# A fused attention and two-MoE kernel: its opening's loads, queue places and low parts rearranged

## The chip, the cores and the metric

The kernel runs on one core of a Trainium2 chip (trn2). The metric is device time in microseconds (us); lower is better. The median of three runs before the change is 1096.28 us (1095.65 to 1096.59).

## The reference

Attention over B = 4 batches, H = 8 heads, S = 576 positions and D = 64, with a memory read beside it, then two gated feed-forward layers on the 2304 x 512 result:

```python
scores = where(causal, -1e9, q @ k.T / sqrt(D)); a = softmax(scores); local = a @ v
q_p = phi(q)                                   # phi(x) = elu(x) + 1
mem_out = (q_p @ M_prev) / (q_p @ z_prev + 1e-6)
x = g * mem_out + (1 - g) * local              # g = sigmoid(beta), one per head
x = (sigmoid(x @ w_gate) * (x @ w_val)) @ w_out       # layer 1: 512 -> 1536 -> 512
out = ((x @ w_a) * (x @ w_b)) @ w_out2                # layer 2: 512 -> 1536 -> 512
```

The feed-forward weights and `setup_inputs` are float64; everything else and the output is float32.

## The kernel before

The attention part works on 16 pairs of heads, four pairs to a batch; pair p is one turn of the loop at L668. A turn interleaves three pairs: the scores, row maxima and exponentials of pair p, the transposes and normalisation of pair p-1, and the product with v of pair p-2. All of it is float32. What a turn does, by function:

- `load_q`, `load_k` (through `load_rows`, L104), `load_v`, `load_z`: three, three, four and one DMA for a pair. Before the loop (L661 to L667) q, k, z and v of pair 0 are loaded and its q and k transposed (`turn`, `turn4`).
- `scores` (L184): six products on TensorE for row blocks X = (0, 2, 3), later six for Y = (1, 4), into one PSUM tile `sc` per head. Y uses the place of X, so it waits until X has been read.
- `expo` (L207): VectorE adds the mask and takes the row extreme (L223), ScalarE takes the exponential with a row sum (L228), GpSimd copies 64 columns of each block into `mix` (L233).
- `phi1` (L239): `e` = exp(min(q, 0)) by VectorE L242 and ScalarE L243, `qp` by VectorE L245, then `e` = qp * z on GpSimd L248. `phi2` (L255): the norm sums on VectorE (L258 to L264). `qp` and `e` have one buffer each.
- `sums` (L267): once all exponentials of pair p-1 are done, VectorE forms the factors (L274, L280, L289) and GpSimd scales `qp` into `mix` (L284, two halves).
- `turn_w`, `turn_mix`, `pv`, `spread`: transposes of the probabilities (tiles `aw`) and of `mix`, products with v, and the way of 1/sum through DRAM back to 64 partitions.

While this runs, layer 1 is prepared. `w_piece` (L389) turns a float64 weight block into float32 and then into a high part (fp32r) and a low part: DMA into `st`; VectorE L402 and ScalarE L406; VectorE L408, L411 and GpSimd L414; ScalarE L417 (high part) and GpSimd L418 (low part). `w_stream` works on 12 such pieces; `fill(p)` (L639) calls one step (two from pair 4 on), three times a turn from p = 1 on. `split_a` (L462) does the same to finished attention columns: ScalarE for the high part, GpSimd L467 for the low. `moe_a` holds the layer-1 matmuls of batches 0 to 2 as small steps of three matmuls (L448 to L450); `M()` puts 12 such steps into a turn once a batch's columns are split and the weights converted. The rest of both layers (from L739) has a fixed order on TensorE.

The order in which each engine's in-order queue is filled is made by a scheduler from the program's order. `with tc.issue_after(x)` keeps what is inside behind instruction x. Two such anchors matter: `st["anchor"]`, the latest score matmul, and `st["pace"]`, the latest row maximum. In the kernel before, weight steps are held behind `pace`.

Of the kernel before, what the change touches and what calls it, by code (L numbers as in the profile page):

```python
# [9 lines left out]
F32 = mybir.dt.float32  # L10
F32R = mybir.dt.float32r
AF = mybir.ActivationFunctionType
ALU = mybir.AluOpType
# [6 lines left out]
def kernel(  # L20
# [82 lines left out]

    def load_rows(t, src, p):  # L104
        b, h = place(p)
        nc.sync.dma_start(
            out=t[:, 0], in_=src[b, h:h + 2, 0:P, :].rearrange("h p d -> p h d")
        )
        for e in H2:
            nc.sync.dma_start(  # L110
                out=t[:, 1:NB, e], in_=src[b, h + e, 64:S, :].rearrange("(i p) d -> p i d", p=P)
            )

# [93 lines left out]
    def expo(p, blocks):  # L207

        wa, wb = width(blocks[-2]), width(blocks[-1])
        both = {}  # L210
        for e in H2:
            if blocks is X_:
                st["mx", p, e] = at.tile([P, NB], F32, tag=f"mx{e}", name="mx")
                st["w", p, e, 0] = at.tile([64, 64], F32, tag="s0", name="s0")
            t = at.tile([P, wa + wb], F32, tag=f"s{blocks[-1]}", name="s", bufs=3)
            st["w", p, e, blocks[-2]], st["w", p, e, blocks[-1]] = t[:, 0:wa], t[:, wa:wa + wb]
            both[e] = t
        for i in blocks:
            w, m = width(i), rows(i)
            c = S - w if i else S - P  # L220
            for e in H2:
                s, mx = st["w", p, e, i], st["mx", p, e]
                st["pace"] = vec.tensor_tensor_reduce(  # L223
                    out=s, in0=scs[e][0:m, SC0[i]:SC0[i] + w], in1=mask[0:m, c:c + w], scale=1.0,
                    scalar=BIG, op0=ALU.add, op1=ALU.min, accum_out=mx[0:m, i:i + 1],
                )
                o = s if i else mix(p)[0:m, 0, e, 64:P]
                act.activation(  # L228
                    out=o, in_=s, func=AF.Exp, scale=-1.0, bias=mx[0:m, i:i + 1],
                    accum_out=sms[p % 2][0:m, i:i + 1, e],  # L230
                )
        for e in H2:
            pool.tensor_copy(  # L233
                out=mix(p)[:, 2:4, e, 64:P] if blocks is X_ else mix(p)[:, 1:NB:3, e, 64:P],
                in_=both[e][:, 0:2 * wa].rearrange("p (i c) -> p i c", i=2)[:, :, 0:64],
            )
# [152 lines left out]
    def w_piece(wsrc, layer, c, kind, src):  # L389
        s = stp.tile([P, 512, 2], I32, tag="st", name="st")  # L390
        w32 = wsrc[kind].bitcast(I32)
        if kind == 2:
            nc.sync.dma_start(out=s.rearrange("p f t -> p (f t)"), in_=w32[c * P:(c + 1) * P, :])
        else:
            nc.sync.dma_start(
                out=s.rearrange("p (a f) t -> p a (f t)", a=KD),
                in_=w32[:, 2 * c * P:2 * (c + 1) * P].rearrange("(a p) f -> p a f", p=P),
            )
        yield
        hi, lo = s[:, :, 1], s[:, :, 0]  # L400
        c32 = work.tile([P, 512], I32, tag="wt", name="wt", bufs=NW)
        vec.tensor_scalar(  # L402
            out=c32.bitcast(F32), in0=hi.bitcast(F32), scalar1=2.0 ** -112, scalar2=None,
            op0=ALU.mult,
        )
        act.activation(out=lo, in_=lo.bitcast(U32), func=AF.Copy, scale=2.0 ** -29)  # L406
        yield
        vec.tensor_scalar(  # L408
            out=c32, in0=c32, scalar1=3, scalar2=None, op0=ALU.logical_shift_left
        )  # L410
        vec.scalar_tensor_tensor(  # L411
            out=c32, in0=hi, scalar=-(1 << 31), in1=c32, op0=ALU.bitwise_and, op1=ALU.bitwise_or
        )
        pool.tensor_tensor(out=c32, in0=c32, in1=lo, op=ALU.add)  # L414
        yield
        t = unit(src, f"w{kind}")
        act.activation(out=t[:, 0], in_=c32.bitcast(F32), func=AF.Copy)  # L417
        pool.tensor_tensor(  # L418
            out=t[:, 1], in0=c32.bitcast(F32), in1=t[:, 0].bitcast(F32), op=ALU.subtract
        )  # L420
        ws[layer, c, kind] = t
        yield
# [39 lines left out]
    def split_a(b, kk):  # L462
# [1 line left out]
        h, l = (xs_a[b, kk][:, i] for i in H2)  # L464
        xk = xb[b, kk][:, 64:S]
        rnd(h, xk, "x" in CD)
        pool.tensor_tensor(out=l, in0=xk, in1=h.bitcast(F32), op=ALU.subtract)  # L467

    def moe_a(b):

# [72 lines left out]
    def start():  # L543
# [5 lines left out]
        )  # L549
        for t in sms:  # L550
            vec.memset(t, 1.0)
        nc.sync.dma_start(
            out=gb, in_=beta.rearrange("(o h) -> o h", o=1).broadcast_to([P, H])
        )
        act.activation(out=og, in_=gb, func=AF.Exp)
# [27 lines left out]
    if True:  # L583
# [55 lines left out]
        def fill(p):  # L639
            settle()  # L640
            split(1)
            if p >= 1:
                with tc.issue_after(st["pace"].ins):
                    for _ in range(1 if p < 4 else 2):
                        w_next()

# [13 lines left out]

        load_q(0)  # L661
        load_k(0)
        load_z(0)
        load_v(0)
        for key in "kq":
            turn(0, key)
        turn4(0)  # L667
        for p in range(NP + 2):  # L668
# [30 lines left out]
            Ms(2)  # L699
            fill(p)  # L700
            if new:
                phi1(p)
                if p:
                    load_v(p)
            if nx:
                load_z(nx)
                for key in "kq":
# [15 lines left out]
            if new:  # L723
                for e in H2:
                    turn_w(p, e, "A")
                phi2(p)
            Ms(2)
            if old is not None:
                Ms()
# [728 lines left out]
```

## Time and profile before

| | before |
|---|---|
| median of three runs | 1096.28 us |
| the profiled execution's own time | 1095.84 us |
| its span | 1094.1 us |
| TensorE matmul busy | 1054.9 us, 96% |
| VectorE busy | 657.5 us, 60% |
| ScalarE busy | 553.6 us, 51% |
| GpSimd busy | 221.3 us, 20% |
| mean granted TensorE clock | 0.994 of full speed |

TensorE is busy for 96% of the span; the 39 us in which it is not lie mostly in the first 150 us, the opening of the attention part. Averages over the whole span therefore say little about this change; the stretches are read one by one. "Idle before" is the time an engine stood still just ahead of an instruction, and the name behind the arrow is what ended it.

### The profile page before, as it was taken

To read this page: it belongs to the slowest core of one execution; us is meant where nothing else is said; L and a number is where in the kernel's file an instruction comes from. 1 tells how busy PE (TensorE), PEld (TensorE's weight loads), DVE (VectorE), ACT (ScalarE), POOL (GpSimd) and SP (SyncE) were. 2 spreads that over 40 slices of the span, in tenths; PEclk is the share of its full clock that TensorE was granted. 3 is DMA by queue.
4 is the path that set the end of the run, shared out by engine and by line. 5 is a ranking of instruction groups with operands and counts; after the bars stand their busy time and mean duration, and the time that the engine had idled before them with its cause. 6 is when DMAs were issued, how large, how long until landed. Compare 5 with 4: busy or idle time off the path is not lost.

```text
span 1094.1 us, 16205 instructions
## 1 busy us (share of the span) xinstructions
PE 1054.9 (96%) x5624; PEld 842.4 (77%) x5624; DVE 657.5 (60%) x1383; ACT 553.6 (51%) x1173; POOL 221.3 (20%) x228
## 2 busy tenths in 40 slices
PE   5887999999999999999999999999999999999998
PEld 3555677677777888888888888888888888888886
DVE  3888765455541988766678464977575568821321
ACT  4877765756742575554556242654443446421221
POOL 2557543142220301110221000221021013200000
PEclk8999999999999999999999999999999999999999
DMA  6555533333113353332358844334233235542233
GB/s 151 137 151 155 143 86 111 87 83 110 38 46 106 112 180 106 130 101 92 123 189 314 269 160 150 130 119 132 73 121 105 93 122 194 190 153 82 83 120 92
DMA packets 147202, 140.61 MB, mean 129 GB/s; under 512 B 73776, under 2 KB 107696, under 8 KB 147120
## 3 DMA queue, kind: packets, MB, share of 16 engines
q1 hardware_dynamic: 147120, 139.58, 40.6%
q8 instruction: 44, 0.72, 0.3%
q14 instruction: 38, 0.31, 0.1%
HBM read 97.00 MB, written 42.54 MB: 128 GB/s over the span
## 4 chain that ended last, share of the span: by engine, by line
PE 75%; DVE 10%; ACT 4%; DMA 3%; POOL 3%; SPq 2%; issue 2%; POOLq 0%; DVEq 0%; ACTq 0%
PE gv L449 14%; PE gv L450 14%; PE gv L448 14%; PE gv L1253 5%; PE gv L1252 4%; PE gv L1251 4%; PE sc L194 3%; PE m L448 3%; PE tp L368 3%; PE m L450 2%; PE m L449 2%; PE tp L329 2%; DVE xm L802 2%; PE tp L342 1%; PE tp L362 1%
## 5 line engine op out<-in xcount | busy, mean ns | idle before, releaser
L449 PE MATMUL gv<-xm,w 128*128 128x512 f32 (+1 forms) x752 | 272.8, 363 | 1.2 <-DVE xm L802 1.2
L448 PE MATMUL gv<-xm,w 128*128 128x512 f32 (+1 forms) x752 | 272.4, 362 | 0.4 <-ACT ev L1066 0.4
L450 PE MATMUL gv<-xm,w 128*128 128x512 f32 (+1 forms) x752 | 272.7, 363 | 0.0
L847 POOL TENSOR_TENSOR wt<-wt,st 128x512 int32<-128x512 int32 x60 | 89.5, 1499 | 528.7 <-DVE wt L843 298.8
L449 PEld LDWEIGHTS gv<-xm,w 128*128 128x128 f32 x752 | 141.5, 188 | 24.2 <-DVE xm L802 1.6
L448 PEld LDWEIGHTS gv<-xm,w 128*128 128x128 f32 x752 | 141.5, 188 | 23.3 <-ACT ev L1066 0.8
L450 PEld LDWEIGHTS gv<-xm,w 128*128 128x128 f32 x752 | 141.6, 188 | 22.0
L1066 ACT ACTIVATE ev<-gv 128x512 f32<-128x512 f32 (+1 forms) x168 | 91.3, 563 | 84.6 <-PE gv L450 84.2
L1070 DVE TENSOR_TENSOR ev<-gv,ev 128x512 f32<-128x512 f32 x120 | 80.6, 684 | 71.6 <-PE gv L450 39.4
L1235 DVE TENSOR_TENSOR gs<-ev,gs 128x512 fp32r<-128x512 f32 (+1 forms) x100 | 63.7, 664 | 51.2 <-ACT gs L1234 49.3
L1234 ACT ACTIVATE gs<-ev 128x512 fp32r<-128x512 f32 (+1 forms) x100 | 56.4, 585 | 73.2 <-DMA ev<-gd 45.5
L1253 PE MATMUL gv<-w,gs 128*128 128x512 f32 x216 | 85.5, 396 | 0.5 <-DVE gs L1235 0.5
L1252 PE MATMUL gv<-w,gs 128*128 128x512 f32 x216 | 85.0, 394 | 0.0
L1251 PE MATMUL gv<-w,gs 128*128 128x512 f32 x216 | 84.2, 390 | 0.0
L228 ACT ACTIVATE s<-s,mx 128x320 f32<-128x320 f32 (+3 forms) x128 | 77.5, 607 | 6.5 <-DVE mx L223 6.5
L148 ACT ACTIVATE aw<-tp 128x512 f32<-128x512 f32 (+2 forms) x112 | 56.3, 513 | 43.4 <-PE tp L329 34.7
L223 DVE CUSTOM_DVE_ANT_0 s<-sc,mask 64x64 f32<-64x64 f32 (+4 forms) x160 | 68.8, 479 | 15.7 <-PE sc L194 15.7
L837 ACT ACTIVATE wt<-st 128x512 f32<-128x512 f32 x60 | 39.5, 667 | 60.5 <-DMA st<-in_moe_w_out_dram 21.2
L194 PE MATMUL sc<-kt,qt 64*128 64x320 f32 (+4 forms) x384 | 61.7, 429 | 1.7 <-DVE mx L223 1.4
L329 PE MATMUL tp<-ident,s 128*128 128x128 f32 x320 | 48.6, 280 | 12.2 <-ACT s L228 5.5
L450 PE MATMUL gv<-gs,w 128*128 128x512 f32 (+1 forms) x160 | 59.7, 373 | 0.0
L449 PE MATMUL gv<-gs,w 128*128 128x512 f32 (+1 forms) x160 | 59.4, 371 | 0.0
(135 smaller groups left out, 1849.0 us busy)
## 6 DMA issues: line engine op xcount, KB each, us to landing
gd<-ev SPq DMA_DIRECT2D x80, 256.0 KB
ev<-gd SPq DMA_DIRECT2D x80, 256.0 KB
st<-in_moe_w_out_dram SPq DMA_DIRECT2D x24, 512.0 KB
st<-in_moe_w_gate_dram SPq DMA_DIRECT2D x12, 512.0 KB
st<-in_moe_w_val_dram SPq DMA_DIRECT2D x12, 512.0 KB
st<-in_moe_w_a_dram SPq DMA_DIRECT2D x12, 512.0 KB
st<-in_moe_w_b_dram SPq DMA_DIRECT2D x12, 512.0 KB
x<-rd SPq DMA_DIRECT2D x32, 144.0 KB
```

What stands on the lines that cost most here:

```text
L194: st["anchor"] = pe.matmul(scs[e][0:m, SC0[i] + a:SC0[i] + z], lhsT=st["q", p][r, r0:r0 + m], rhs=st["k", p][r, a:z], start=True, stop=True,)
L228: act.activation(out=o, in_=s, func=AF.Exp, scale=-1.0, bias=mx[0:m, i:i + 1], accum_out=sms[p % 2][0:m, i:i + 1, e],)
L329: pe.transpose(out=t[:, c:c + P], in_=st["w", p, e, i][:, P * j - 64:P * j + 64], identity=ident)
L448: pe.matmul(o, lhsT=w[:, 0, ws_], rhs=xh, start=first, stop=False, skip_group_check=True)
L449: pe.matmul(o, lhsT=w[:, 0, ws_], rhs=xl, start=False, stop=False, skip_group_check=True)
L450: return pe.matmul(o, lhsT=w[:, 1, ws_], rhs=xh, start=False, stop=last, skip_group_check=True)
L847: pool.tensor_tensor(out=c32, in0=c32, in1=lo, op=ALU.add)
L1066: act.activation(out=t[:, 0:n], in_=src[:, 0:n], func=func)
L1070: st["gate"] = vec.tensor_tensor(out=t, in0=src, in1=t, op=ALU.add)
L1251: pe.matmul(o, lhsT=t[:, 0, r], rhs=w[:, 0], start=first, stop=False)
L1252: pe.matmul(o, lhsT=t[:, 0, r], rhs=w[:, 1], start=False, stop=False)
L1253: st["gate"] = pe.matmul(o, lhsT=t[:, 1, r], rhs=w[:, 0], start=False, stop=last)
```

## The change

Four things are done, all to the attention part.

- The three DMAs of k for pair 0 are issued by ScalarE's queue instead of SyncE's, so is the DMA of `beta`, which moves out of `start` into a new function `start2`, with the exponentials and scalings of the gate, called after `load_k(0)`. The loads of z and v of pair 0 move from ahead of the loop into turn 0, behind the loads of q and k of pair 1.
- Weight steps are held behind `st["apace"]`, the latest exponential, as well as behind `st["pace"]`.
- `phi2` (norm sums) is held behind `st["pace"]`, the latest row maximum.
- The low parts of `w_piece` and `split_a` move from GpSimd to VectorE.

```diff
--- before.py
+++ after.py
@@ -103,11 +103,12 @@
 
     def load_rows(t, src, p):
         b, h = place(p)
-        nc.sync.dma_start(
+        q_ = nc.scalar if p == 0 and src is k else nc.sync
+        q_.dma_start(
             out=t[:, 0], in_=src[b, h:h + 2, 0:P, :].rearrange("h p d -> p h d")
         )
         for e in H2:
-            nc.sync.dma_start(
+            q_.dma_start(
                 out=t[:, 1:NB, e], in_=src[b, h + e, 64:S, :].rearrange("(i p) d -> p i d", p=P)
             )
 
@@ -225,7 +226,7 @@
                     scalar=BIG, op0=ALU.add, op1=ALU.min, accum_out=mx[0:m, i:i + 1],
                 )
                 o = s if i else mix(p)[0:m, 0, e, 64:P]
-                act.activation(
+                st["apace"] = act.activation(
                     out=o, in_=s, func=AF.Exp, scale=-1.0, bias=mx[0:m, i:i + 1],
                     accum_out=sms[p % 2][0:m, i:i + 1, e],
                 )
@@ -415,7 +416,7 @@
         yield
         t = unit(src, f"w{kind}")
         act.activation(out=t[:, 0], in_=c32.bitcast(F32), func=AF.Copy)
-        pool.tensor_tensor(
+        vec.tensor_tensor(
             out=t[:, 1], in0=c32.bitcast(F32), in1=t[:, 0].bitcast(F32), op=ALU.subtract
         )
         ws[layer, c, kind] = t
@@ -464,7 +465,7 @@
         h, l = (xs_a[b, kk][:, i] for i in H2)
         xk = xb[b, kk][:, 64:S]
         rnd(h, xk, "x" in CD)
-        pool.tensor_tensor(out=l, in0=xk, in1=h.bitcast(F32), op=ALU.subtract)
+        vec.tensor_tensor(out=l, in0=xk, in1=h.bitcast(F32), op=ALU.subtract)
 
     def moe_a(b):
 
@@ -549,7 +550,8 @@
         )
         for t in sms:
             vec.memset(t, 1.0)
-        nc.sync.dma_start(
+    def start2():
+        nc.scalar.dma_start(
             out=gb, in_=beta.rearrange("(o h) -> o h", o=1).broadcast_to([P, H])
         )
         act.activation(out=og, in_=gb, func=AF.Exp)
@@ -640,7 +642,7 @@
             settle()
             split(1)
             if p >= 1:
-                with tc.issue_after(st["pace"].ins):
+                with tc.issue_after(st["pace"].ins), tc.issue_after(st["apace"].ins):
                     for _ in range(1 if p < 4 else 2):
                         w_next()
 
@@ -660,8 +662,7 @@
 
         load_q(0)
         load_k(0)
-        load_z(0)
-        load_v(0)
+        start2()
         for key in "kq":
             turn(0, key)
         turn4(0)
@@ -699,9 +700,10 @@
             Ms(2)
             fill(p)
             if new:
+                if not p:
+                    load_z(0)
                 phi1(p)
-                if p:
-                    load_v(p)
+                load_v(p)
             if nx:
                 load_z(nx)
                 for key in "kq":
@@ -723,7 +725,8 @@
             if new:
                 for e in H2:
                     turn_w(p, e, "A")
-                phi2(p)
+                with tc.issue_after(st["pace"].ins):
+                    phi2(p)
             Ms(2)
             if old is not None:
                 Ms()
```

Line numbers of the changed kernel are higher by one to three. The order in which the instructions stand on an engine shows three places. In these names `s` and `mx` are the score block and its row extreme (sm_93 belongs to even pairs, sm_94 to odd ones), `st` and `wt` the weight block, `w_436` and `w_620` the first two converted pieces, `xs` the split columns.

ScalarE, pair 0, from the last exponentials of the X blocks to those of Y, before:

```order
L228 ACTIVATE s,sm_93<-s,mx 128x448
L165 ACTIVATE kt<-tp 128x128
L228 ACTIVATE s,sm_93<-s,mx 128x448
L406 ACTIVATE st<-st 128x512 x2
L228 ACTIVATE s,sm_93<-s,mx 128x192 x2
L148 ACTIVATE aw<-tp 128x512
L228 ACTIVATE s,sm_93<-s,mx 128x576
L148 ACTIVATE aw<-tp 128x512
L228 ACTIVATE s,sm_93<-s,mx 128x576
```

The same place in the change, and then pair 1 in the change, at its X and Y exponentials:

```order
L229 ACTIVATE s,sm_93<-s,mx 128x448
L166 ACTIVATE kt<-tp 128x128
L229 ACTIVATE s,sm_93<-s,mx 128x448
L229 ACTIVATE s,sm_93<-s,mx 128x192 x2
L149 ACTIVATE aw<-tp 128x512
L229 ACTIVATE s,sm_93<-s,mx 128x576
L149 ACTIVATE aw<-tp 128x512
L229 ACTIVATE s,sm_93<-s,mx 128x576
```

```order
L229 ACTIVATE s,sm_94<-s,mx 128x320
L229 ACTIVATE s,sm_94<-s,mx 128x448 x2
L407 ACTIVATE st<-st 128x512
L229 ACTIVATE s,sm_94<-s,mx 128x192
L149 ACTIVATE aw<-tp 128x512
L229 ACTIVATE s,sm_94<-s,mx 128x192
```

The two L406 steps on `st` that stood ahead of pair 0's 192-wide exponentials are gone from there; the first one stands behind pair 1's 448-wide ones, ahead of pair 1's 192-wide one.

VectorE, from the scaling of q^T of pair 0 to the first row maxima, before:

```order
L161 TENSOR_SCALAR qt<-tp 128x448
L161 TENSOR_SCALAR qt<-tp 128x128
L258 TENSOR_REDUCE nr<-e 128x10
L259 SCALAR_TENSOR_TENSOR nr<-nr,gb 128x10
L264 RECIPROCAL nr<-nr 128x10
L242 TENSOR_SCALAR e<-qn 128x640
L223 ISA s_178,mx<-sc,mask 64x64
L223 ISA mx 64x1
L223 ISA s_181,mx<-sc,mask 64x64
L223 ISA mx 64x1
L223 ISA s,mx<-sc,mask 128x320
```

In the change, the same place, and then the place behind pair 0's last row maxima:

```order
L162 TENSOR_SCALAR qt<-tp 128x448
L246 SCALAR_TENSOR_TENSOR qp<-qn,e 128x640
L560 TENSOR_SCALAR og<-og 128x8
L560 TENSOR_SCALAR gb<-gb 128x8
L162 TENSOR_SCALAR qt<-tp 128x128
L224 ISA s_170,mx<-sc,mask 64x64
L224 ISA mx 64x1
L224 ISA s_173,mx<-sc,mask 64x64
```

```order
L224 ISA s,mx<-sc,mask 128x576
L224 ISA mx 128x1
L259 TENSOR_REDUCE nr<-e 128x10
L260 SCALAR_TENSOR_TENSOR nr<-nr,gb 128x10
L243 TENSOR_SCALAR e<-qn 128x640
L265 RECIPROCAL nr<-nr 128x10
L275 SCALAR_TENSOR_TENSOR t<-sm_93,og 128x10
```

The norm sums of pair 0 (nr) and the minimum of pair 1 (e<-qn) stood ahead of the first row maxima and now stand behind the last ones of pair 0.

GpSimd in pairs 1 and 2, before and in the change:

```order
L414 TENSOR_TENSOR wt<-wt,st 128x512
L233 COPY mix<-s 128x2x64 x2
L284 TENSOR_TENSOR mix<-qp,nr 128x6x64
L284 TENSOR_TENSOR mix<-qp,nr 128x4x64
L418 TENSOR_TENSOR w_436<-wt,w_436 128x512
L248 TENSOR_TENSOR e<-qp,zb 128x640
L233 COPY mix<-s 128x2x64
L467 TENSOR_TENSOR xs<-x,xs 128x512
L233 COPY mix<-s 128x2x64
L414 TENSOR_TENSOR wt<-wt,st 128x512
```

```order
L234 COPY mix<-s 128x2x64 x3
L415 TENSOR_TENSOR wt<-wt,st 128x512
L234 COPY mix<-s 128x2x64
L285 TENSOR_TENSOR mix<-qp,nr 128x6x64
L285 TENSOR_TENSOR mix<-qp,nr 128x4x64
L249 TENSOR_TENSOR e<-qp,zb 128x640
L234 COPY mix<-s 128x2x64 x2
L415 TENSOR_TENSOR wt<-wt,st 128x512
L234 COPY mix<-s 128x2x64 x2
```

The rows `w_436<-wt,w_436` and `xs<-x,xs` are gone from GpSimd (24 such rows in the whole attention part: 12 weight pieces, 12 column blocks); they stand on VectorE now.

## Rows read from the trace of the kernel before

**Rows 1.** Pair to pair: length, busy PE, PEld, DVE, ACT, POOL; PEclk, DMA, GB/s.

```profile
8.13:23.13 15.00, 8.17 (x46) 4.93 (x46) 6.91 (x27) 7.13 (x24) 1.66 (x3) 0.90 0.94 217
23.13:35.34 12.21, 10.16 (x58) 6.20 (x57) 8.79 (x33) 8.74 (x28) 4.14 (x7) 0.84 0.27 62
35.34:50.15 14.81, 13.92 (x105) 9.22 (x106) 12.76 (x40) 13.10 (x39) 9.03 (x11) 1.00 0.49 126
50.15:63.08 12.93, 11.38 (x99) 8.15 (x98) 10.68 (x37) 10.66 (x32) 8.57 (x11) 1.00 0.67 170
63.08:81.57 18.49, 14.86 (x102) 9.57 (x102) 14.01 (x43) 13.99 (x40) 10.37 (x13) 0.91 0.61 162
81.57:101.30 19.73, 14.83 (x109) 10.01 (x108) 17.37 (x44) 12.75 (x37) 13.69 (x15) 1.00 0.53 149
101.30:126.19 24.89, 23.44 (x151) 17.36 (x150) 20.48 (x49) 20.58 (x46) 12.61 (x15) 1.00 0.46 133
126.19:145.97 19.78, 18.77 (x128) 12.63 (x129) 13.04 (x41) 15.62 (x41) 12.14 (x14) 1.00 0.53 148
145.97:166.75 20.78, 20.78 (x140) 15.06 (x141) 11.78 (x36) 13.63 (x38) 10.96 (x13) 1.00 0.30 78
```

**Rows 2.** Timeline from 0 to 25 us: start, length, engine, line, operation, [idle before <-releaser].

```profile
0.73 0.40 SPq L552 DMA_DIRECT2D gb<-in_beta_dram  x1
...
2.72 0.51 SPq L106 DMA_DIRECT2D kn<-in_k_dram  x1
...
5.56 0.45 PE L169 MATMUL tp<-ident,kn 128*128 128x128 f32 x1 [5.56 <-DMA kn<-in_k_dram]
...
7.54 0.51 SPq L106 DMA_DIRECT2D qn<-in_q_dram  x1
...
8.13 2.61 PE L194 MATMUL sc<-kt,qt 64*64 64x64 f32 x12 [0.21 <-ACT kt L165]
...
11.34 0.49 DVE L242 TENSOR_SCALAR e<-qn 128x640 f32<-128x640 f32 x1 [0.82 <-DMA qn<-in_q_dram]
...
11.75 0.21 DVE L223 CUSTOM_DVE_ANT_0 s<-sc,mask 64x64 f32<-64x64 f32 x1
...
14.46 1.05 SPq L395 DMA_DIRECT2D st<-in_moe_w_gate_dram  x2
...
15.56 0.66 ACT L228 ACTIVATE s<-s,mx 128x448 f32<-128x448 f32 x1
...
19.30 0.65 ACT L406 ACTIVATE st<-st 128x512 int32<-128x512 uint32 x1 [2.99 <-DMA st<-in_moe_w_gate_dram]
...
21.70 0.44 ACT L228 ACTIVATE s<-s,mx 128x192 f32<-128x192 f32 x1
```

**Rows 3.** Timeline from 25 to 50 us, VectorE around the maxima of pair 1.

```profile
25.18 0.17 DVE L274 SCALAR_TENSOR_TENSOR t<-sm,og 128x10 f32<-128x10 f32 x1 [7.29 <-ACT s L228]
...
27.82 0.21 DVE L223 CUSTOM_DVE_ANT_0 s<-sc,mask 64x64 f32<-64x64 f32 x1
...
31.82 0.80 DVE L258 TENSOR_REDUCE nr<-e 128x10 f32<-128x640 f32 x1
...
33.30 0.35 DVE L223 CUSTOM_DVE_ANT_0 s<-sc,mask 128x192 f32<-128x192 f32 x1
```

**Rows 4.** Chain of waits between 35.34 and 146 us, its shares by line.

```profile
by line: issue 9.0%; POOL w L418 7.5%; PE sc L194 6.5%; DVE s L223 6.5%; POOL mix L284 5.6%; DVE wt L411 5.3%; POOL wt L414 4.7%; POOL e L248 4.2%; DVE qp L245 3.9%; DMA st<-in_moe_w_out_dram 3.2%; DVE aw L146 3.0%; ACT s L228 3.0%; PE m L4
```

**Rows 5.** Lines L418 and L802, count: duration in ns min/median/max, first and last start.

```profile
L418 POOL TENSOR_TENSOR w<-wt,w x12: 1264/1274/1298, 39.7 to 132.7; 128x512 fp32r<-128x512 f32 x12
...
L802 DVE TENSOR_TENSOR w<-wt,w x60: 673/682/1197, 383.1 to 944.0; 128x512 fp32r<-128x512 f32 x60
```

**Rows 6.** VectorE by shape, 35.3 to 146 us: count, busy us, mean ns, idle before.

```profile
L411 DVE SCALAR_TENSOR_TENSOR wt<-st,wt 128x512 int32<-128x512 int32 x12 | 11.6, 965 | 0.2
```

**Rows 7.** Timeline near 101.6 us, GpSimd and VectorE at once.

```profile
101.54 1.27 POOL L418 TENSOR_TENSOR w<-wt,w 128x512 fp32r<-128x512 f32 x1 [0.20 <-ACT w L417]
...
101.69 1.67 DVE L411 SCALAR_TENSOR_TENSOR wt<-st,wt 128x512 int32<-128x512 int32 x1
```

## The prediction, made before the changed kernel was run

> **What bounds the kernel now.** I read the busy times by stretch first, cut where the first scores of each pair of heads start [rows 1]. From 145.97 us on, one pair takes 20.78 us and TensorE is busy for all of it: work and time are the same there, and nothing on another engine shortens it. Before that TensorE is not full: the first pair takes 15.00 us with 8.17 us of matmuls, the second 12.21 with 10.16, and the six from 35.34 to 145.97 together 110.63 us with 97.2 us. The change touches only the attention part, so a gain must come from these 138 us. Once the matmuls run without a gap, everything behind them follows earlier by what the opening saves, because the number of matmuls stays the same.
>
> Then the timeline of the first 25 us [rows 2]. Three waits follow one another. First, k of pair 0 is issued at 2.72 us, behind beta and q, and TensorE starts at 5.56. Second, the scores start at 8.13, but the first row maximum only at 11.75: in VectorE's queue the minimum of pair 1 stands ahead of it, and that waited for q of pair 1, issued at 7.54. Third, the X exponentials of pair 0 end at 16.22 (15.56 + 0.66), and the next ones, of Y, start at 21.70: the weight steps L406 stand between them, and the first waited 2.99 us for its DMA and began at 19.30. From there the path goes on through the sums of pair 0 (25.18) to the row maxima of pair 1 at 27.82 [rows 3].
>
> Last the chain of waits from 35.34 to 146 us, by line [rows 4]: no engine owns it. GpSimd's low part of the weights, L418, has 7.5% of it, GpSimd's L284, L414 and L248 together 14.5%.
>
> **The change part by part.**
>
> *A, until pair 1's maxima.* k now has a queue of its own. Its issue can start where beta's did, at 0.73, so 1.99 us earlier. The scores gain between 0 and that; I take 1.6, since the gate's exponentials now stand ahead of the copy of k^T on ScalarE. So scores at 6.5. The five DMAs for z and v of pair 0 no longer stand ahead of q and k of pair 1 on SyncE, so these are issued several us before 7.54; z and v are wanted later (v two turns later), and the norm product on GpSimd, which needs z, is off the path until the sums. With the norm sums behind the maxima, the first maximum needs only the first score, say 0.5 us later: 7.0 instead of 11.75, 4.75 earlier. The scores themselves take 2.61 us, so the last X maximum now waits for the last score; that takes back about 0.45. And without the two weight steps the Y exponentials follow the X ones directly: 21.70 - 16.22 = 5.5 us. Sum 4.75 - 0.45 + 5.5 = **9.8 us**, which should put the maxima of pair 1 at 18.0 instead of 27.82. If the earlier maxima gave nothing, 5.5 would be left; if nothing were taken back, 10.3.
>
> *What is moved past what.* The first L406 now stands behind pair 1's 448-wide exponentials. Its DMA was issued at 14.46 and landed by 19.30, 4.8 us later [rows 2]. It is issued a little earlier now, so it lands by about 17 to 19, and ScalarE reaches it near 22. Costed at nothing, with a cover of 3 us or more; without the cover it is a rival below.
>
> *B, pair 1.* VectorE did its norm sums and the next minimum from 31.82 to 33.30 ahead of the Y maxima [rows 3]; they now come behind, where it otherwise waits for exponentials. 33.30 - 31.82 = **1.5 us**. Between 0 (the waits just change places) and 3.4 (VectorE's whole idle time in that stretch, 12.21 - 8.79 [rows 1]).
>
> *C, pairs 2 to 7.* All 12 weight pieces and the 4 column blocks of batch 0 have their low parts here. GpSimd took 1.27 us for one, VectorE takes 0.68 for the same operation and size elsewhere (L802) [rows 5]. VectorE has room on paper: it is busy for 88.3 of 110.6 us, and 16 x 0.68 = 10.9 makes 99.2. The 7.5% of L418 on the chain is 8.3 us; with 0.68 in place of 1.27 it is 4.4, a gain of 3.9. The column blocks do not show on the chain's leading lines; I take nothing for them. Bounds: at best all the visible idle of TensorE in these six pairs goes, 13.4 us [rows 1]. At worst every low part lies on the path, at the mean of the two-input L411, 0.965 us [rows 6]: 16 x 0.965 = 15.4 us lost. I take **4 us**: it lies in the middle of a wide range, and nearest to the chain's own rows.
>
> A row speaks against this part. L411, which reads two operands from SBUF, took 1.67 us when it started 0.15 us behind GpSimd's L418, which took 1.27 [rows 7]; 0.68 is what such an instruction takes alone. So either engine can hold the other, and the moved low parts have two such operands. The Trainium skill, in "SBUF — State Buffer", section "Who interferes with whom", has it as a rule: a VectorE instruction with two inputs in SBUF contends with a GpSimd instruction that reads SBUF, and the one that comes second waits for the whole of the other. This trace agrees, as said. By that rule alone the 16 low parts cost up to 16 x 1.67 = 26.7 us of VectorE and C would be a loss; against it stands that the same 16 leave GpSimd, so fewer are left to collide with (L418 was the other party in rows 7). I keep C at 4; rival 3 takes the collisions up.
>
> *D, the rest.* In pairs 8 to 15 TensorE has no gap, so 8 more low parts moved there change nothing; VectorE, at 11.78 of 20.78 us [rows 1], has the room. Behind the attention part nothing is changed.
>
> **Sum.** 9.8 + 1.5 + 4 = 15.3, say 15 us. The profiled execution took 1095.84 us (span 1094.1); less 15 that is **1081 us**. The median of the runs is 1096.28, 0.44 above it, so against the median the gain is about 1.4%. A measurement of this kernel can tell 0.2%, about 2.2 us, from no change.
>
> **The rivals.**
>
> 1. *The opening only.* The stall at 16.22 goes, but the freed time is lost again in pairs 1 to 7, where VectorE's added 10.9 us and GpSimd's relief cancel: A alone, 5.5 to 9.8, gives 1086 to 1090. For it: VectorE is at 17.37 of 19.73 us in pair 5 [rows 1]. Against: four of the chain's top eight lines are GpSimd's.
> 2. *The slack comes out.* If shorter queues let TensorE run through from pair 2 on, C is 9 to 13 and the time 1068 to 1076. For it: pairs 4 and 5 alone hold 8.5 us of TensorE idle; against: VectorE would have to run at over 95% there.
> 3. *Slower: VectorE's queue becomes the path.* Its maxima feed everything, and its in-order queue now has 16 low parts between them, each waiting for ScalarE's high part and able to be held by GpSimd. All on the path at 0.965 they cost 15.4 us, against 11.3 of A and B: 1095.84 + 4.1 = about 1100. It decides from the point where more than 11.3 us of them is on the path, 12 of the 16. Against: VectorE was idle for 22.3 us in these pairs. The rule of the Trainium skill named under C ("SBUF — State Buffer") speaks for this rival; the rows do not show how often the two engines will meet.
> 4. *The stall only moves.* Should the weight block land after ScalarE reaches L406 in pair 1, the Y exponentials of pair 1 wait as those of pair 0 did, up to 5.5 us: about 1086. Its DMA must then take some 3 us longer than before.
> 5. *No change*, within 2.2 us of 1095.84: rival 3 with just as much lost as won.
>
> **How the numbers follow.** Forecast (1076 to 1086) 0.50; opening only 0.20; slack out 0.12; stall moves 0.08; no change 0.03; slower 0.07. The likeliest case gives 1081. The range takes A from 5.5 with B and C at nothing (1090.3) to A 10.3, B 3.4 and C 9 (1073.1): 1073 to 1091. Outside lie rivals 3 and 5 and the lower half of rival 2, some 0.16. Faster by over 0.2%: 0.50 + 0.20 + 0.12 + 0.08 = 0.90; within 0.03; slower 0.07.
>
> **What would show it.** Right: the first row maximum at about 7 us, no L406 ahead of pair 0's 192-wide exponentials, pair 1's maxima at 18, the granted clock without the dip that the first two stretches show (0.90 and 0.84 [rows 1]), and the first gapless pair beginning some 15 us earlier, near 131. Wrong in A: ScalarE waiting for the weight DMA in pair 1, or the first scores not before 8. Wrong in C: VectorE over 95% busy from pair 2 on with low parts well above 0.68 us, or TensorE waiting for a weight's low part in pairs 5 to 7.

## The result, and the profile after

The changed kernel took **1083.52 us** (median of four runs, 1080.91 to 1087.03); the kernel before, run beside it, 1096.43. The ratio is **0.9885 [0.9853, 0.9918]**, a gain of 12.9 us (9.0 to 16.1 by the interval) where 15.3 were forecast. The profiled execution took 1085.2 us, its span is 1083.4; all stretches and timelines below come from one profiled execution of each kernel.

Stretch by stretch after the change, cut as [rows 1] from score start to score start (length; busy PE, PEld, DVE, ACT, POOL; PEclk, DMA, GB/s):

```profile
7.79:16.55 8.76, 7.33 (x46) 4.73 (x45) 5.62 (x27) 5.51 (x21) 2.13 (x3) 1.00 0.75 181
16.55:29.05 12.50, 10.00 (x57) 6.34 (x58) 8.89 (x33) 9.16 (x29) 4.12 (x7) 0.86 0.65 155
29.05:45.13 16.08, 14.04 (x106) 9.46 (x105) 15.60 (x49) 14.16 (x42) 8.75 (x12) 0.95 0.59 157
45.13:59.16 14.03, 12.90 (x98) 8.69 (x98) 11.71 (x35) 10.83 (x32) 5.58 (x7) 0.93 0.54 141
59.16:74.01 14.85, 12.59 (x103) 8.53 (x102) 14.73 (x45) 13.13 (x39) 6.80 (x10) 1.00 0.66 170
74.01:96.84 22.83, 21.30 (x126) 14.84 (x125) 19.98 (x55) 15.64 (x42) 10.28 (x13) 0.85 0.57 157
96.84:117.91 21.07, 20.34 (x139) 15.18 (x138) 17.21 (x49) 18.47 (x41) 9.31 (x10) 1.00 0.57 164
...
137.07:157.85 20.78, 20.78 (x138) 15.07 (x137) 14.05 (x41) 13.64 (x38) 7.83 (x11) 1.00 0.30 78
```

Pair 0 takes 8.76 us instead of 15.00, pair 1 12.50 instead of 12.21. Pairs 2 to 7 end at 137.07 instead of 145.97: 108.0 us instead of 110.6. The gapless stretch begins 8.8 us earlier (before, its first scores start at 145.90, 0.07 us ahead of the cut in [rows 1]); the rest of the gain lies behind it. In pairs 2 and 4 VectorE is now busy for 15.60 of 16.08 and 14.73 of 14.85 us.

The timeline of the opening, columns as in [rows 2]:

```profile
3.29 0.45 PE L170 MATMUL tp<-ident,kn 128*128 128x128 f32 x1 [3.29 <-DMA kn<-in_k_dram]
...
5.65 0.49 DVE L243 TENSOR_SCALAR e<-qn 128x640 f32<-128x640 f32 x1 [4.74 <-DMA qn<-in_q_dram]
...
7.79 2.60 PE L195 MATMUL sc<-kt,qt 64*64 64x64 f32 x12
...
10.55 0.22 DVE L224 CUSTOM_DVE_ANT_0 s<-sc,mask 64x64 f32<-64x64 f32 x1 [2.29 <-PE sc L195]
...
14.90 0.46 ACT L229 ACTIVATE s<-s,mx 128x192 f32<-128x192 f32 x1 [0.34 <-DVE mx L224]
...
20.29 0.83 DVE L246 SCALAR_TENSOR_TENSOR qp<-qn,e 128x640 f32<-128x640 f32 x1 [1.27 <-POOL mix L285]
...
21.04 0.21 DVE L224 CUSTOM_DVE_ANT_0 s<-sc,mask 64x64 f32<-64x64 f32 x1
...
24.94 0.65 ACT L407 ACTIVATE st<-st 128x512 int32<-128x512 uint32 x1
```

Against [rows 2] and [rows 3]: the first transpose of k starts 2.27 us earlier (5.56 to 3.29), the scores 0.34 us (8.13 to 7.79), the first maximum 1.20 us (11.75 to 10.55), the Y exponentials 6.80 us (21.70 to 14.90), pair 1's maxima 6.78 us (27.82 to 21.04). The first weight step L407 comes in pair 1, with no wait ahead of it.

The instruction that the change moved in every pair is the norm reduction. The view of its one line (operation and count: duration in ns min/median/max, first and last start; then how long VectorE stood idle in front of it, and how often) says, before, up to 146 us:

```profile
L258 DVE TENSOR_REDUCE nr<-e x8: 799/819/822, 9.2 to 135.5; 128x10 f32<-128x640 f32 x8
its engine sat idle before it (us, times) until:
  POOL e L248: 6.1, 5
```

The same view after:

```profile
L259 DVE TENSOR_REDUCE nr<-e x8: 809/812/815, 16.4 to 134.2; 128x10 f32<-128x640 f32 x8
its engine sat idle before it (us, times) until:
who waited for it (us, times):
```

Before, VectorE waited five times at the head of its queue for GpSimd's product, 6.1 us in all; now never. The prediction has no term for these waits.

The moved low parts and their neighbour after the change, 29 to 140 us (count, busy us, mean ns, idle before):

```profile
L419 DVE TENSOR_TENSOR w<-wt,w 128x512 fp32r<-128x512 f32 x12 | 10.4, 867 | 3.8 <-ACT w L418 3.8
...
L412 DVE SCALAR_TENSOR_TENSOR wt<-st,wt 128x512 int32<-128x512 int32 x12 | 8.8, 737 | 0.0
```

A weight's low part takes 0.87 us on the mean (0.69 in the median, 1.55 at most); its neighbour fell from 0.965 [rows 6] to 0.737. In front of the low parts VectorE waited 3.8 us for ScalarE's high part. Pair 6 shows the longest of these waits, on VectorE's timeline:

```profile
97.38 0.81 DVE L246 SCALAR_TENSOR_TENSOR qp<-qn,e 128x640 f32<-128x640 f32 x1
100.47 0.96 DVE L419 TENSOR_TENSOR w<-wt,w 128x512 fp32r<-128x512 f32 x1 [2.28 <-ACT w L418]
101.36 0.21 DVE L224 CUSTOM_DVE_ANT_0 s<-sc,mask 64x64 f32<-64x64 f32 x1
```

### The profile page after: what moved, and what is told of

The parts are those of the page before. It is cut to its first block, busy times and chain, and to the rows that moved or that the text cites. A ratio compares the mean times of both kernels' runs of the same rounds, so it can differ in the third digit from the quotient of the medians.

```text
span 1083.4 us, 16215 instructions
## 1 busy us (share of the span) xinstructions
PE 1055.7 (97%) x5624; PEld 844.6 (78%) x5624; DVE 664.9 (61%) x1407; ACT 552.2 (51%) x1173; POOL 193.6 (18%) x204
## 4 chain that ended last, share of the span: by engine, by line
PE 82%; DVE 8%; ACT 3%; DMA 3%; issue 1%; POOL 1%; SPq 1%; POOLq 0%; DVEq 0%; ACTq 0%
PE gv L450 16%; PE gv L451 16%; PE gv L449 15%; PE gv L1256 5%; PE gv L1255 5%; PE gv L1254 4%; PE sc L195 4%; PE m L449 3%; PE tp L369 3%; PE m L451 3%; PE m L450 3%; PE tp L330 2%; PE tp L343 2%; DVE s L224 2%; PE tp L363 1%
## 5 line engine op out<-in xcount | busy, mean ns | idle before, releaser
L451 PE MATMUL gv<-gs,w 128*128 128x512 f32 (+1 forms) x160 | 59.6, 373 | 0.0
L450 PE MATMUL gv<-gs,w 128*128 128x512 f32 (+1 forms) x160 | 59.4, 371 | 0.0
L449 PE MATMUL gv<-gs,w 128*128 128x512 f32 (+1 forms) x160 | 58.9, 368 | 0.0
```

The costliest lines, as they stand in the source:

```text
L449: pe.matmul(o, lhsT=w[:, 0, ws_], rhs=xh, start=first, stop=False, skip_group_check=True)
L450: pe.matmul(o, lhsT=w[:, 0, ws_], rhs=xl, start=False, stop=False, skip_group_check=True)
L451: return pe.matmul(o, lhsT=w[:, 1, ws_], rhs=xh, start=False, stop=last, skip_group_check=True)
```

## The experiments

All kernels compute the full result. The kernel before, run beside each group, had a median of 1096.43, 1096.98, 1097.29 and 1096.93 us, so a difference between kernels of two groups can be off by up to 0.9 us. The change's own median comes from four runs and its interval is 3.6 us to either side; every "above the change" below carries that.

### Each part undone

`u_a`: the weight steps wait for the maxima alone.

```diff
-                with tc.issue_after(st["pace"].ins), tc.issue_after(st["apace"].ins):
+                with tc.issue_after(st["pace"].ins):
```

> The change, but the weight steps wait again for the row maxima alone, not for the exponentials (L407 may stand ahead of pair 0's Y exponentials on ScalarE). Theory (the 5.5 us in which ScalarE stood at the weight step are the largest part of the gain): Y exponentials of pair 0 again near 20 us, pair 1's maxima near 26 instead of 21.04, and 5 to 6 us of the 12.9 us between the medians are lost: 1088 to 1091. Rival (the time freed there is made up later anyway, and the low parts carry the gain): 1083 to 1086, as the change.

Measured 1089.96 us, ratio 0.9941 [0.9929, 0.9953]: 6.4 us above the change. Its interval lies clear of the change's. Pair 0's Y exponentials come at 21.16 and pair 1's maxima at 27.28, each some 1.2 us later than the theory had them. ScalarE's timeline has the stall back:

```profile
19.01 0.65 ACT L407 ACTIVATE st<-st 128x512 int32<-128x512 uint32 x1 [3.60 <-DMA st<-in_moe_w_gate_dram]
...
21.16 0.44 ACT L229 ACTIVATE s<-s,mx 128x192 f32<-128x192 f32 x1
```

The theory holds: what is won at the stall is kept to the end.

`u_b`: both low parts on GpSimd again.

```diff
-        vec.tensor_tensor(
+        pool.tensor_tensor(
             out=t[:, 1], in0=c32.bitcast(F32), in1=t[:, 0].bitcast(F32), op=ALU.subtract
...
-        vec.tensor_tensor(out=l, in0=xk, in1=h.bitcast(F32), op=ALU.subtract)
+        pool.tensor_tensor(out=l, in0=xk, in1=h.bitcast(F32), op=ALU.subtract)
```

> The change, but both low parts (weights and column blocks) are again on GpSimd. Theory of the prediction (C): pairs 2 to 7 take about 4 us longer than in the change, whose stretch from 29.05 to 137.07 was 108.0 us; time 1086 to 1089. Rival 1 of the prediction (VectorE's load and GpSimd's relief cancel): 1082 to 1086, no difference. Rival 3 (low parts cost on VectorE, which is busy for 95 to 99% of several pairs now): faster than the change, 1076 to 1081.

Measured 1086.01 us, 0.9904 [0.9891, 0.9917]: 2.5 us above the change, but the interval overlaps the change's own. Pairs 1 to 4 run faster with the low parts on GpSimd (pair 5 starts at 70.99 instead of 74.01), pairs 5 to 7 together slower (pair 8 at 138.47 instead of 137.07). Most of what they lose lies in pair 5, which took 26.48 us at a granted clock of 0.76 instead of 22.83 at 0.85. The time lies at the lower edge of the first theory's range; the third theory is out, the second is not, because of the overlap.

`u_c`: the loads as before.

```diff
-        q_ = nc.scalar if p == 0 and src is k else nc.sync
...
-    def start2():
-        nc.scalar.dma_start(
+        nc.sync.dma_start(
...
-        start2()
+        load_z(0)
+        load_v(0)
...
```

> The change, but with the loads as before: k of pair 0 and beta on SyncE's queue, beta first, z and v of pair 0 ahead of q and k of pair 1. Theory after the trace (the scores came only 0.34 us earlier, since q landed later when k was issued beside it): the loads are worth 0.3 to 1.5 us, 1084 to 1086. Rival (the prediction's step A: 1.6 us of it from the scores, and q and k of pair 1 early enough for the minimum): 3 us or more, 1086 to 1089.

Measured 1084.63 us, 0.9887 [0.9872, 0.9903]: no difference from the change that can be told. Its scores start at 8.32 instead of 7.79, pair 8 even 0.24 us earlier than in the change. The theory holds, at its lower end: undoing the loads alone costs nothing that can be told.

`u_d`: the norm sums without the wait.

```diff
-                with tc.issue_after(st["pace"].ins):
-                    phi2(p)
+                phi2(p)
```

> The change, but the norm sums (the reduction, the two that follow it) are again free to stand ahead of the row maxima. Theory after the trace (the first maximum waits for the last of the six scores, not for the queue): worth 1 us or less, 1083 to 1086. Rival (the prediction's A and B: 4.75 us at the first maximum with the loads, 1.5 us in pair 1): 1085 to 1090, with a first maximum at 11 us or later and row maxima of pair 1 later by 1.5 us or more than 21.04.

Measured 1093.03 us, 0.9975 [0.9964, 0.9986]: **9.5 us** above the change, more than either theory gave. VectorE's timeline in pair 0:

```profile
12.00 0.82 DVE L259 TENSOR_REDUCE nr<-e 128x10 f32<-128x640 f32 x1 [3.64 <-POOL e L249]
...
13.50 0.15 DVE L224 CUSTOM_DVE_ANT_0 s<-sc,mask 64x64 f32<-64x64 f32 x1
```

The scores had started at 7.89 and taken 2.41 us, so they were done at 10.30; the maximum came at 13.50, behind a sum that stood at the queue's head for 3.64 us. GpSimd's product, on which that sum waits, started only at 10.43, when the later load of z was there; with the old loads (`u_c`) it starts at 7.84. Pair 1's maxima come at 25.11. So the theory fell, and the rival had the places right: of the parts undone alone, the wait of the norm sums costs the most.

### Is that wait worth something by itself?

`u_cd`: the change with the edits of `u_c` and `u_d`, so weight steps and low parts alone.

> The change without its loads and without the wait of the norm sums: weight steps behind the exponentials and low parts on VectorE alone. Undone alone, the loads cost nothing and the wait of the norm sums 9.5 us. Theory (the loads bring z of pair 0 later, so GpSimd's product comes later and the norm sums, heading VectorE's queue, hold the first maximum to 13.50 us instead of 10.55; the wait only repairs that): with the old loads the wait is not needed, first maximum at 11 to 12 us, time 1083 to 1087. Rival (norm sums ahead of the maxima cost time in every pair, whatever the loads): 1090 to 1094, and pairs 2 to 7 longer than the 108.0 us of the change by 3 us or more.

Measured 1091.57 us, 0.9951 [0.9939, 0.9964]. The rival holds in its time: against `u_c` the wait is worth 6.9 us with the old loads too. Its other sign was missed narrowly: pairs 2 to 7 are 2.6 us longer than in the change, where it asked for 3 or more. The same view of the norm reduction in this kernel:

```profile
L258 DVE TENSOR_REDUCE nr<-e x9: 801/820/822, 9.4 to 144.2; 128x10 f32<-128x640 f32 x9
its engine sat idle before it (us, times) until:
  POOL e L248: 4.0, 4
```

Its pairs 2 to 7 take 142.24 - 31.61 = 110.6 us, the time of before, although the low parts are on VectorE and the weight steps wait for the exponentials.

`o_d`: the kernel before with this one part.

```diff
-                phi2(p)
+                with tc.issue_after(st["pace"].ins):
+                    phi2(p)
```

> The kernel before with one part of the change: the norm sums wait for the row maxima. Theory (the wait repairs what the loads do, and the stall at the weight step of pair 0 stays): 1094 to 1097, no difference. Rival (the norm sums are in the way by themselves, the prediction's B and part of A): 1087 to 1093, and pair 1's maxima earlier than 27.82 by 1.5 us or more.

Measured 1092.95 us, 0.9963 [0.9950, 0.9976]: 4.0 us faster than before, which the theory excluded. The rival has the time right and the place wrong: pair 1's maxima come at 27.53 instead of 27.82, since the stall at the weight step (19.09 us) is still there; the gain lies in pairs 1 to 7. Pairs 2 to 7 take 142.36 - 34.05 = 108.3 us.

The stretch from pair 2's first scores to pair 8's holds the same matmuls in these kernels (685 or 686 records), so its length can be compared. The views of it, columns as above, for `before`, `o_d`, `u_b`, `u_cd`, `u_d`, the change and `u_c`:

```profile
35.34:145.97 110.63, 97.21 (x686) 66.94 (x688) 88.33 (x249) 86.71 (x229) 66.43 (x76) 0.98 0.54 147
34.05:142.36 108.31, 97.56 (x685) 66.54 (x685) 90.01 (x253) 86.93 (x228) 68.94 (x75) 0.98 0.56 150
28.27:138.47 110.20, 101.61 (x686) 69.96 (x685) 89.32 (x253) 87.10 (x229) 66.80 (x75) 0.94 0.54 147
31.61:142.24 110.63, 99.24 (x686) 67.74 (x685) 95.64 (x265) 86.33 (x229) 50.03 (x60) 0.97 0.57 147
33.81:146.35 112.54, 100.59 (x686) 68.76 (x685) 95.27 (x265) 86.46 (x229) 49.94 (x60) 0.95 0.56 145
29.05:137.07 108.02, 98.65 (x685) 68.72 (x685) 92.63 (x268) 87.11 (x230) 48.66 (x58) 0.95 0.56 151
28.83:136.83 108.00, 99.12 (x685) 68.72 (x685) 91.52 (x268) 86.85 (x230) 48.46 (x58) 0.95 0.58 153
```

Length, and behind it how much of it TensorE stood still (length less busy PE):

| low parts on | norm sums free | norm sums behind the maxima |
|---|---|---|
| GpSimd | 110.6, 13.4 (before) | 108.3, 10.8 (`o_d`); 110.2, 8.6 (`u_b`) |
| VectorE | 110.6, 11.4 (`u_cd`); 112.5, 12.0 (`u_d`) | 108.0, 9.4 (the change); 108.0, 8.9 (`u_c`) |

Three pairs of kernels differ in the norm sums alone: before and `o_d`, `u_d` and the change, `u_cd` and `u_c`. Held back, they take 2.5 to 2.7 us off TensorE's gaps each time, whichever engine has the low parts; the lengths fall by 2.3, 4.5 and 2.6 us. The low parts alone are compared by `u_b` and the change. With them on GpSimd the gaps are not larger (8.6 against 9.4 us); the stretch is 2.2 us longer because the same matmuls took 101.6 us instead of 98.7, at a clock of 0.94 instead of 0.95. So in these executions the low parts on VectorE closed no gap. How far two executions of one kernel differ in this stretch was not measured.

### Which low part, and when?

`u_b2` puts the low parts of the column blocks back on GpSimd:

```diff
-        vec.tensor_tensor(out=l, in0=xk, in1=h.bitcast(F32), op=ALU.subtract)
+        pool.tensor_tensor(out=l, in0=xk, in1=h.bitcast(F32), op=ALU.subtract)
```

> The change, but the low parts of the four column blocks are again on GpSimd, those of the 12 weights stay on VectorE. Undoing both cost some 2 us. Theory of the prediction (the weights' low parts carry C, the column blocks nothing): as the change, 1081 to 1084. Rival (the column blocks, which the first expert matmuls wait for, carry it): 1085 to 1088.

`u_b1` does it with those of the weights:

```diff
-        vec.tensor_tensor(
+        pool.tensor_tensor(
             out=t[:, 1], in0=c32.bitcast(F32), in1=t[:, 0].bitcast(F32), op=ALU.subtract
...
```

> The change, but the low parts of the 12 weights are again on GpSimd, those of the four column blocks stay on VectorE. Undoing the column blocks alone cost 3 us, undoing both the same. Theory (the column blocks carry C, the weights' low parts cost VectorE as much as they save: in the change the first maximum of pair 6 comes at 101.36, 2.7 us after its scores, behind a low part that waited for its high part): as the change or up to 3 us faster, 1080 to 1084, and pair 6's first maximum within 1 us of its scores' end. Rival of the prediction (the weights carry C): 1085 to 1088.

Measured 1086.89 us, 0.9912 [0.9899, 0.9925], and 1087.34 us, 0.9917 [0.9903, 0.9932]. By the medians either half undone costs 3.4 to 3.8 us, both together 2.5. Both rivals' times came, though each gives the whole to another half, and both intervals overlap the change's: the runs do not tell which half, if any, carries a gain. Pair 6's first maximum in `u_b1` comes at 102.78 with scores from 100.32, so the wait of 2.28 us is gone as expected, and yet the kernel is not faster.

`v_late`: GpSimd up to pair 4, VectorE from pair 5 on (`now` is the loop's p).

```diff
-        vec.tensor_tensor(
+        (pool if st['now'] < 5 else vec).tensor_tensor(
...
```

> The change, but low parts are on GpSimd up to pair 4 and on VectorE from pair 5 on. With all of them on GpSimd pair 5 began 3.0 us earlier than in the change (70.99 against 74.01) and pair 8 1.4 us later. Theory (VectorE's queue is the limit up to pair 4, GpSimd's from pair 5 on): both gains together, pair 5 at 71 to 72, pair 8 at 134 to 136, time 1080 to 1082. Rival (the earlier pair 5 only finds its weights later, so nothing is kept): pair 8 at 137 to 139, time 1083 to 1086.

Measured 1083.44 us, 0.9883 [0.9867, 0.9899]. Pair 5 starts at 72.00 and pair 8 at 135.40, as the theory said, but its time of 1080 to 1082 was missed and the median is the change's. The two profiled executions do keep the lead, 1.7 us at pair 8, to the end (1083.44 against 1085.20), but the medians do not show it: inconclusive at this size of effect.

### One more instruction behind the maxima

`v_phi`: from pair 1 on, L246 waits for the maxima as well.

```diff
-        vec.scalar_tensor_tensor(
-            out=qp, in0=qn, scalar=0.0, in1=e, op0=ALU.max, op1=ALU.add
-        )
+        with tc.issue_after(st["pace"].ins) if p else ExitStack():
+            vec.scalar_tensor_tensor(
+                out=qp, in0=qn, scalar=0.0, in1=e, op0=ALU.max, op1=ALU.add
+            )
```

> The change and one more of the same kind: from pair 1 on, the sum of maximum and exponential (L246, 0.82 us, which waits until GpSimd has read the buffer of the pair ahead) waits for the X row maxima too. In the change it stands ahead of the maxima of pairs 1 and 8, which come 2.7 and 1.5 us after the scores' end. Theory (an instruction that waits on GpSimd must not stand ahead of the maxima in VectorE's queue): pair 1's first maximum at 18.5 to 19.5 instead of 21.04, time 1079 to 1082. Rival (VectorE is full from pair 2 on, the instruction only stands elsewhere): 1082 to 1086.

Measured 1093.17 us, 0.9960 [0.9948, 0.9972]: 9.7 us slower than the change, so both theory and rival fell. Pair 1's maxima do come at 19.61 instead of 21.04, but pairs 3 and 4 take 17.6 and 18.3 us instead of 14.0 and 14.9. Here are the two pairs, columns as above, and VectorE in pair 4:

```profile
44.41:62.00 17.59, 15.31 (x110) 10.41 (x109) 12.19 (x39) 11.38 (x33) 5.51 (x7) 0.88 0.40 111
62.00:80.26 18.26, 15.78 (x103) 10.30 (x102) 16.51 (x45) 13.80 (x41) 8.00 (x10) 0.79 0.57 140
```

```profile
70.43 0.81 DVE L247 SCALAR_TENSOR_TENSOR qp<-qn,e 128x640 f32<-128x640 f32 x1
...
71.63 1.79 DVE L469 TENSOR_TENSOR xs<-x,xs 128x512 fp32r<-128x512 f32 x1
...
74.14 0.68 DVE L420 TENSOR_TENSOR w<-wt,w 128x512 fp32r<-128x512 f32 x1
74.75 0.34 DVE L224 CUSTOM_DVE_ANT_0 s<-sc,mask 128x192 f32<-128x192 f32 x1
```

Why it is slower stays open. The moved instruction is the last reader of q's buffer, and SyncE's load of a following q does start only behind it, at 71.27. The profile's chain of waits runs through that load to the maximum at 74.75. But VectorE was at work without a gap up to that maximum, and the list of waits of this kernel from 28.77 to 148.34 us has none for a load of q on any engine. What the traces show instead is that most of the added time of pairs 3 and 4 is longer matmul time: 15.31 and 15.78 us busy at clocks of 0.88 and 0.79, where the change has 12.90 and 12.59 at 0.93 and 1.00 (the first of the two with 12 more matmuls, the second with as many). GpSimd also waited longer for `qp` ahead of its product: 9.7 us between 29 and 100 us, against 1.9 in the change.

### The steps of the opening

`k_seq`: k of pair 0 through SyncE again, behind q; beta stays on ScalarE.

```diff
-        q_ = nc.scalar if p == 0 and src is k else nc.sync
-        q_.dma_start(
+        nc.sync.dma_start(
...
```

> The change, but k of pair 0 goes through SyncE's queue behind q (beta stays on ScalarE's): k is issued 1.5 us later than in the change, q alone. Theory (k and q issued side by side share the DMA engines, so q lands 0.8 us later than before): VectorE's first minimum, which waits for q, begins at 4.4 to 5.0 us instead of 5.65, the first scores at 7.5 to 8.1, time as the change, 1081 to 1086. Rival (q lands late for a reason of its own): the minimum still at 5.5 or later, the scores at 8.5 or later.

Measured 1083.80 us, 0.9889 [0.9871, 0.9908]. The timeline:

```profile
2.30 0.51 SPq L106 DMA_DIRECT2D kn<-in_k_dram  x1
...
4.93 0.49 DVE L242 TENSOR_SCALAR e<-qn 128x640 f32<-128x640 f32 x1 [0.84 <-DMA qn<-in_q_dram]
...
8.05 2.18 PE L194 MATMUL sc<-kt,qt 64*64 64x64 f32 x12
```

With k issued 1.57 us later (2.30 instead of 0.73), VectorE has q at 4.93 instead of 5.65, and the scores start 0.26 us later. One trace a kernel is little for that: the four with the old loads, all alike in the opening, have q at 4.83, 5.11, 5.22 and 5.43. But from q's issue to VectorE's minimum it is 3.6 to 4.2 us in these four and `k_seq`, where k follows q, and 4.8 to 5.0 us in all nine with k beside q. The theory holds: side by side, k's transfer slows q's. The Trainium skill has the rule in "DMA: Bandwidth & Descriptors", section "Issuing engines are not separate DMA queues": transfers started by several engines run on the same 16 DMA engines, and only the time to issue them is saved. These traces agree: k's issue comes 1.57 us earlier, and q is there later for it.

`v_pipe`: scores and maxima block by block.

```diff
         for i in blocks:
+            scores(p, (i,))
             w, m = width(i), rows(i)
...
-                scores(p, X_)
                 expo(p, X_)
```

(the same for Y).

> The change, but each block's scores are followed by its maxima and exponentials in the program, where the change writes all scores of X (or Y) first. Theory (in the change the first maximum carries one wait, for the sixth score, and the other five maxima have none, so it cannot start with the first score as the prediction's A took it): the first maximum now needs two scores and comes at 8.4 to 9.2 us instead of 10.55, with scores at 7.7 to 7.9. The scores of a head share one PSUM tile, so each later block of scores now waits for the maxima ahead of it, and the last X maximum comes no earlier; time not below the change: 1083 to 1092. Rival (the wait does not matter, VectorE's queue holds the first maximum): first maximum at 10 us or later. Rival (the maxima's start is the path, as A has it): last X maximum of pair 0 earlier by 1 us or more than 12.2, time 1079 to 1082.

Measured 1103.61 us, 1.0050 [1.0032, 1.0068], 20 us slower than the change. VectorE's timeline in pair 0:

```profile
8.30 0.22 DVE L225 CUSTOM_DVE_ANT_0 s<-sc,mask 64x64 f32<-64x64 f32 x1 [0.17 <-PE sc L195]
...
13.07 0.62 DVE L225 CUSTOM_DVE_ANT_0 s<-sc,mask 128x448 f32<-128x448 f32 x1
```

The first maximum now follows the first scores (7.66 + 0.48) at 8.30, the last starts at 13.07 instead of 12.21. In these places the theory holds; the time is far outside its range (1083 to 1092), and where most of the 20 us arises was not traced. In the change the first maximum carries the only wait for TensorE, and it covers all six scores, as VectorE's order with its waits shows:

```
9 L224 ISA s_170,mx<-sc,mask 64x64 [waits PE_49,Pool_49]
10 L224 ISA mx 64x1
11 L224 ISA s_173,mx<-sc,mask 64x64
12 L224 ISA mx 64x1
13 L224 ISA s,mx<-sc,mask 128x320
```

No version tried beats the change by more than the intervals.

## Why the prediction was right, and where not

The time lies in the range and in the likeliest case (1076 to 1086); the sum was 2.4 us too high against the medians, which is inside the interval, and 4.7 us against the profiled executions (1095.84 - 1085.2 = 10.6). In these the lead is 6.8 us at pair 1's maxima, 6.3 at pair 2's scores (35.34 to 29.05), 8.8 at pair 8's and 10.7 at the end. That the total came so near is in part luck: A was 3 us too large, and the size of C was met by a part that the prediction had not priced. The 0.2% that it took for the least difference that can be told was too little; the change's interval is 0.33% to either side.

**A, 9.8 us forecast, 6.8 measured.** *Scores at 6.5* came at 7.79: the step took k's issue time and left q where it was, but q landed 0.8 us later than in the trace before (0.2 to 0.8 against all four with the old loads), because k was moved beside it (`k_seq`); with k early, TensorE waited for q instead. *First maximum at 7.0, 4.75 earlier* is the step that failed: it came at 10.55, 1.20 earlier. "The first maximum needs only the first score" does not hold for this program; its wait covers the sixth. Already before, the scores ended at 8.13 + 2.61 = 10.74, so the queue's share of the wait until 11.75 was 1.0 us, which [rows 2] could have told. *The stall, 5.5*: 6.80 - 1.20 = 5.6 measured, and `u_a` pays 6.4 us for having it back. *The weight step past the exponentials, at nothing*: right, L407 at 24.94 has no wait; rival 4 is out. *The loads*, credited with part of A, are worth nothing that can be told (`u_c`).

**B, 1.5 us in pair 1, measured -0.3** by score starts (12.50 instead of 12.21) and -1.0 by maxima (32.92 - 21.04 = 11.88 instead of 38.73 - 27.82 = 10.91). The step itself was right: the Y maxima no longer stand behind the norm sums. They now wait for their scores:

```profile
24.22 2.71 PE L195 MATMUL sc<-kt,qt 64*128 64x192 f32 x12
...
26.98 0.36 DVE L224 CUSTOM_DVE_ANT_0 s<-sc,mask 128x192 f32<-128x192 f32 x1 [1.87 <-PE sc L195]
```

The six scores took 2.71 us at a granted clock of 0.57, against 1.57 us at 1.00 in the trace before (from 30.65). In `u_c` and `u_b`, which have the same wait, pair 1 ran at 1.00 throughout, the scores took 1.57 us, and the pair 11.0 us: 1.2 us less than before by score starts, 0.5 by maxima. What the step left out is that the clock can fall just there.

**C, 4 us in pairs 2 to 7 from the low parts, measured 2.6, mostly from another cause.** The failed step is the attribution: it read L418's 7.5% of the chain as time that comes back. With the low parts on VectorE and the norm sums free the stretch took 110.6 us as before (`u_cd`); with the norm sums held it took 108.3 with the low parts still on GpSimd (`o_d`). The norm sums of the later pairs were priced nowhere. VectorE stood still for them for 6.1 us before, and the whole wait is worth 4.0 us alone and 9.5 us beside the other parts. TensorE's gaps in the stretch did shrink by 4.0 us (13.4 to 9.4), as much as forecast, but its matmuls took 1.4 us longer (97.2 to 98.7) at a clock of 0.95 instead of 0.98. Undone, the low parts cost 2.5 us by the medians (`u_b`); nothing at all lies inside the change's own interval, too. The collisions weighed under C came seldom: L419 took 0.69 us in the median and 0.87 on the mean, and up to 1.55, not 1.67 each time. Part of rival 3 did come: VectorE above 95% busy in pairs 2 and 4, and maxima behind a low part in pair 6.

**D, nothing.** The lead grows from 8.8 us at pair 8 to 9.7 at pair 15's scores (294.78 to 285.10) and 10.7 at the end of the span; the last 1.0 us was not traced to a place.

Undone one at a time the parts cost 6.4, 2.5, 1.1 and 9.5 us, together 19.5, while the change gains 12.9. That would mean that the parts lean on each other, which a sum over parts, as the prediction made it, cannot show. But the change's median enters that sum four times: were it 2.2 us higher, still inside its interval, the two would agree. The nearer sign is the wait of the norm sums, 4.0 us alone and 9.5 beside the others; how the parts share the gain is otherwise open.

## What to carry to other kernels

In an in-order queue, look for the instruction that waits for another engine ahead of those on which everything else hangs, and read how long the engine stood in front of it in every turn, not only in the first. Holding such an instruction back is not always a gain: with the norm sums it gave 4.0 to 9.5 us, with `qp` it lost 9.7, for a reason that is not shown. A chain of waits may name a load although the engine behind it was never idle; read that engine's timeline too. Compare the busy time of the same matmuls before a longer stretch is put down to waits. And read what a wait covers: a maximum that waits for the last of six scores does not start with the first.

## What the runs showed of the hardware that was not expected

The granted clock did not lose its dips, as the prediction said it would: before, two stretches of [rows 1] lie well below full (0.84 and 0.91, beside 0.90 in the first); after, 0.86, 0.95, 0.93 and 0.85 in pairs 1, 2, 3 and 5, so TensorE ran part of each at its lower level of 1.2 GHz. The pairs ahead of the two deepest have gaps (pair 0: busy 7.33 of 8.76 us; pair 4: 12.59 of 14.85), and the stretch without gaps from 137.07 on has 1.00. Gaps alone do not settle it: before, pair 5 was busy for 14.83 of 19.73 us, and it and pair 6 have 1.00. The four runs of the change go with their mean granted clock: 0.997 and 1080.91 us, 0.996 and 1081.84, 0.993 and 1085.20, 0.990 and 1087.03. In other kernels they go together less well (`u_b` has 0.998 at 1083.68 and at 1086.01). That one sets the other was not tried; it would explain why the interval of the change is so wide, and why effects of 2 to 3 us could not be told apart here.
